# Moving dK/dV matmuls and the turns inside the attention backward loop

## The chip, the cores and the metric

The kernel runs on one core of a Trainium2 chip. The metric is the device time of one execution in microseconds, as the median of several runs. One execution was also recorded by the hardware profiler; the durations and waits quoted here come from that one.

## The reference

The reference computes a transformer block with conditioned layer norms and all its gradients: x has 2048 tokens of width 512, attention has 32 heads of width 16 without a mask, the dense part has 1792 hidden features with a squared ReLU. It returns the output and nine gradients. The change touches only the attention backward pass, which for every head computes, from the queries, keys, values and the gradient of the head's output dO:

```
P  = exp(scale * Q K^T)            (2048 x 2048 per head)
dP = dO V^T  (less the row term)    dS = P * dP
dV = P^T dO      dK = dS^T Q * scale      dQ = dS K * scale
```

The row normalisation and the row term of the softmax gradient are folded into dO before this stage: dO arrives divided by the row sums, and two more columns of dO and V carry the row term. So dS is one plain product of dP and P.

## The kernel before, in words

The kernel has three stages: the forward pass with the dense part worked in between, the attention backward pass (`attn_bwd`, from about 1170 to 2401 us of the profiled span), and the last weight gradients. Only the second is changed.

**Loops.** `attn_bwd` goes over 8 groups of four heads (`g`) and two pairs of heads in each (`jp`); one (g, jp) is called a pass here, and there are 16. A pass goes over four blocks of 512 keys (`c`), and for each over 16 blocks of 128 queries (`ib`). One (c, ib) is a unit: the two heads of the pair, 128 queries by 512 keys. Four consecutive units make a group (`i` from 0 to 3), so that a pass has 64 units and 16 groups, and the stage 1024 units. The units of a group are called first to fourth below.

**One unit.** For each of the two heads `a`, TensorE computes the scores into a one-bank PSUM tile `st` (L1584), and beside them the dP of the unit before into a tile `dp` (L1509). The two use different halves of the array's rows (64 rows each). `stp` and `dpp` have three banks each. ScalarE takes the exponential of the scores to `pu` (L1587); VectorE multiplies `dp` by the `pu` of the same unit to `ds` (L1513). Six `pu` buffers exist.

**What follows a unit.** `dS` (L1524) appends the unit to the list `pend`; when a group is complete, it issues one DMA transpose of the group's `ds` to `dsT` on SP (L1530) and appends eight dQ pieces to `pendq`. Four kinds of work are taken from lists and placed by hand between the units:

- dK and dV: `kv` (L1449) issues four matmuls with 128 contraction rows and 16 output columns each, running side by side in the array, that add to one PSUM bank `acckv`, and `kv_two` (L1494) calls it for the two oldest units. It is called at the end of the second and fourth unit of each group. When a block of keys is complete (ib 15), ScalarE evicts `acckv` to `kvT` (L1458). The next block starts a new accumulation in the same bank. Counting with the lists, the last unit of a block is worked off at the end of the fourth unit of the next block's first group.
- dQ: `dq` (L1474), 16 matmuls at the end of the first and third unit of a group, from the `dsT` of a group about two groups back. With the last piece of a pass, VectorE scales the accumulator to `dqT` (L1483).
- Turns: `turn` (L1460) transposes half of `kvT` on TensorE (8 transposes into one `st` bank, L1468) and ScalarE copies the result to `dk_t` and `dv_t` (L1472); `turn_q` (L1486) does the same for dQ (4 transposes, L1491, one copy, L1492). Both wait in the list `turnq`; one entry is taken before the second unit of a group. In an ordinary pass the three turns of the pass before fall in groups 1, 2 and 3.
- dS transposes: `turn_ds` (L1535), in even groups, transposes an eighth of the group's `ds` on TensorE and ScalarE (L1543, L1544) in place of the DMA.

**Odd groups.** `off` (L1515) holds in odd groups. There one of the eight multiplies of VectorE (second unit, second head) is left out: ScalarE copies that `dp` to SBUF (L1521) and POOL multiplies (L1522). `turn_ds` moves no data in these groups.

**What sets the order.** On TensorE, SP and POOL the instructions run in the order in which the code issues them; ScalarE's and VectorE's order in this stage follows the code as well, by the trace. So a call that is moved in the code moves in TensorE's queue. The condition on dK/dV stands in two lines:

```python
if i % 2 == 1 and len(pend) >= 4:
    kv_two()
```

When a second or fourth unit starts, `pend` has four entries, and three after `kv_two` has run; this lag is the same before and after the change.

Of the kernel before, what the change touches and what calls it, by code (L numbers as in the profile page):

```python
# [105 lines left out]
class K:  # L106
# [1322 lines left out]
    def attn_bwd(self):  # L1429
# [8 lines left out]
        S, D, H, NQ, ST, SC = self.S, self.D, self.H, self.NQ, self.ST, self.SC  # L1438
# [8 lines left out]
        pend, pendq, turnq = [], [], []  # L1447

        def kv(u):  # L1449
            (T, g, jp, c, ib, kvT, pu, ds) = u  # L1450
            for j, (n, src) in enumerate((("Q", ds), ("dO", pu))):
                for a in range(2):
                    r = 64 * j + 32 * a
                    col = (2 * jp + a) * DH
                    nc.tensor.matmul(acckv[r:r + DH, :], lhsT=T[n][:, ib, col:col + DH], rhs=src[:, a, :],  # L1455
                                     start=(ib == 0), stop=(ib == ST - 1))
            if ib == ST - 1:
                nc.scalar.activation(kvT[:, 512 * c:512 * (c + 1)], acckv[:], ACT.Copy, scale=kvs[:])  # L1458

        def turn(g, jp, kvT, s0):  # L1460

            if kvT is None:
                return turn_q(g, jp)
            h0 = 4 * g + 2 * jp
            n = ST // 2
            tp = stp.tile([P, n, P], BF16, name="st")
            for st in range(n):
                nc.tensor.transpose(tp[:, st, :], kvT[:, (s0 + st) * P:(s0 + st + 1) * P], self.ident[:])  # L1468
            v = tp[:].rearrange("p s (t a e) -> p t s a e", t=2, a=2)
            for t, dst in enumerate((self.dk_t, self.dv_t)):  # L1470
                d = dst[:, s0:s0 + n, h0 * DH:(h0 + 2) * DH].rearrange("p s (a d) -> p s a d", a=2)
                nc.scalar.copy(d, v[:, t, :, :, 0:DH])  # L1472
# [19 lines left out]
            nc.scalar.copy(self.dq_t[:, :, h0 * DH:(h0 + 2) * DH], tp[:].rearrange("p b (i e) -> p (b i) e", i=G))  # L1492

        def kv_two(n=2):  # L1494
            for u in pend[2 - n:2]:
                kv(u)
            (T, g, jp, c, ib, kvT, pu, ds) = pend[1]
            del pend[:2]
            if c % 2 and ib == ST - 1 and (g, jp) == (NQ - 1, 1):
                turnq.append((g, jp, kvT, 4 * (c - 1)))  # L1500
            elif c == SC - 1 and ib == ST - 1:
                turnq.extend((g, jp, kvT, s0) for s0 in (0, ST // 2))

        def dP(u, a):

            (T, g, jp, c, ib, kvT, pu, dsg, i, grp) = u
            rd = slice(64 - 64 * jp, 128 - 64 * jp)
            dp = dpp.tile([P, 512], F32, name="dp")
            nc.tensor.matmul(dp[:], lhsT=T["dOT"][rd, ib * P:(ib + 1) * P],  # L1509
                             rhs=masked["VT"][a][rd, 512 * c:512 * (c + 1)], start=True, stop=True)  # L1510
            if a == 1 and i == 1 and off(c, ib):
                return dp
            nc.vector.tensor_tensor(dsg[:, i, a], dp[:], pu[:, a, :], ALU.mult)  # L1513

        def off(c, ib):  # L1515
            return (c * SC + ib // G) % 2 == 1

        def dP_pool(u, dp):
            (T, g, jp, c, ib, kvT, pu, dsg, i, grp) = u
            f = (self.junk6, self.csq)[(c * SC + ib // G) // 2 % 2]  # L1520
            nc.scalar.copy(f[:], dp[:])  # L1521
            nc.gpsimd.tensor_tensor(dsg[:, i, 1], f[:], pu[:, 1, :], ALU.mult)  # L1522

        def dS(u):  # L1524

            (T, g, jp, c, ib, kvT, pu, dsg, i, grp) = u
            pend.append((T, g, jp, c, ib, kvT, pu, dsg[:, i]))
            if i == G - 1:
                dsT, n = grp
                nc.sync.dma_start_transpose(dsT[:, n:, :], dsg[:].rearrange("p i a k -> p (i a k)")[:, n * P:])  # L1530
                for a in range(2):
                    for sub in range(4):
                        pendq.append((T, g, jp, c, ib - G + 1, a, sub, dsT))
# [13 lines left out]
        T = self.T0  # L1547
        last = None
        for g in range(NQ):
            for jp in range(2):  # L1550
                if jp == 0:
                    if g + 1 < NQ:
                        Tn, later = self.load_group(g + 1)
                    else:
                        Tn, later = None, self.wq_pieces(1) + self.load_wmt()
                    cut = len(later) // 2 if Tn else len(later)
                    pieces = self.pair_pieces(g, 1) + later[:cut]
                    later = later[cut:]
                elif g + 1 < NQ:
                    pieces = self.pair_pieces(g + 1, 0) + later  # L1560
                else:
                    pieces = [(self.xhat1_6[:, st, :], self.xhat1_d.rearrange("(st p) d -> p st d", p=P)[:, st, :])
                              for st in range(ST)]
                kvT = kvp.tile([P, S], BF16, name="kvT")
                total = len(pieces)
                for c in range(SC):
                    c0 = 512 * c
                    for ib0 in range(0, ST, G):
                        m = c * (ST // G) + ib0 // G
                        while pieces and (total - len(pieces)) * SC * ST <= m * G * total:  # L1570
                            if last:
                                nc.gpsimd.tensor_copy(tick[:], last[7][0:1, 0, 0, 0:1])
                            nc.gpsimd.dma_start(*pieces.pop(0))
                        dsg, grp = self.dsp.tile([P, G, 2, 512], BF16, name="ds"), []
                        for i in range(G):
                            ib = ib0 + i
                            q = slice(ib * P, (ib + 1) * P)
                            if turnq and i == 1:
                                turn(*turnq.pop(0))
                            pu = self.pup.tile([P, 2, 512], BF16, name="pu")  # L1580
                            for a in range(2):
                                stt = stp.tile([P, 512], F32, name="st")
                                rs = slice(64 * jp, 64 * jp + 64)
                                nc.tensor.matmul(stt[:], lhsT=T["QT"][rs, q], rhs=masked["KT"][a][rs, c0:c0 + 512],  # L1584
                                                 start=True, stop=True)
                                held = dP(last, a) if last else None
                                nc.scalar.activation(pu[:, a, :], stt[:], ACT.Exp, scale=self.scale)  # L1587
                                if held is not None:
                                    dP_pool(last, held)
                            if last:  # L1590
                                dS(last)
                            last = (T, g, jp, c, ib, kvT, pu, dsg, i, grp)
                            if i % 2 == 1 and len(pend) >= 4:
                                kv_two()
                            elif i % 2 == 0 and len(pendq) > 4 * G:
                                for _ in range(8 if len(pendq) > 6 * G else 4):
                                    dq(pendq.pop(0))
                            if i == 2:
                                turn_ds(dsg, grp, off(c, ib))
            T = Tn  # L1600
        with tc.manual_schedule(engines=ALL):
            for t in (2, 0):
                for p in self.wq_pieces(t):
                    nc.gpsimd.dma_start(*p)
            for a in range(2):
                dP(last, a)
            dS(last)
            while len(pend) > 2:
                kv_two()
            kv(pend[0])  # L1610
            for _ in range(2 * G):
                dq(pendq.pop(0))
            kv_two(1)
            k0, v0, k1 = [dpp.tile([P, 512], F32, name="dp") for _ in range(3)]
            self.dw_mm(k0, 1, 0, 0, ST // 2)
            turn(*turnq.pop(0))
            for _ in range(2 * G):
                dq(pendq.pop(0))
            self.dw_mm(v0, 2, 0, 0, ST // 2)
            self.dw_mm(k0, 1, 0, ST // 2, ST)  # L1620
            self.col_sum(1)
            self.dw_mm(v0, 2, 0, ST // 2, ST)
            self.col_sum(2)
            self.cs_bc(1)
            while pendq:
                dq(pendq.pop(0))
            self.cs_bc(2)
            turn(*turnq.pop(0))
            self.dw_mm(k1, 1, 1, 0, ST)
# [312 lines left out]
```

## Time and profile before

| what | value |
|---|---|
| median of 3 runs | 2526.64 us (2521.6 to 2527.84) |
| the profiled execution's own time | 2524.31 us |
| its span, first to last instruction | 2522.4 us |
| TensorE busy | 2433.1 us, 96% of the span |
| VectorE busy | 1705.4 us, 68% |
| ScalarE busy | 2296.2 us, 91% |
| POOL busy | 713.9 us, 28% |
| multiplies dS = P dP on VectorE (L1513) | 1920, mean 681 ns |
| exponentials of the backward stage (L1587) | 2048, mean 641 ns |
| POOL's multiplies (L1522) | 128, mean 1151 to 1154 ns |

In the profile L and a number name a line of the kernel; an instruction is written as output<-inputs. PE is TensorE, PEld its weight loads, DVE is VectorE, ACT is ScalarE, SP issues the DMA transposes. The mean time of one instruction includes its overlap with the next: two multiplies in a row start closer together than 681 ns. A matmul's end is modelled, its start is recorded. In the order of time a line gives the start and the length in us, and several instructions of one kind in a row are merged and counted with x.

### The profile page before, as it was taken

How to read it: one execution, taken by the hardware profiler on the slowest of the kernel's cores; microseconds unless marked ns; L12 is line 12 of the kernel's file. 1: busy time of each engine (PE TensorE's matmuls, PEld its weight loads, DVE VectorE, ACT ScalarE, POOL GpSimd, SP SyncE). 2: the span in 40 equal slices, each digit the busy share in tenths (PEclk: the TensorE clock that was granted, in tenths of full speed). 3: DMA queues.
4: the chain of work that ended last, by engine and by line, in shares of the span. 5: the costliest groups of instructions: out<-in, count | busy, mean ns of one | idle time of the engine just before them, and what ended most of it. 6: DMA issues, size and time to landing. Idle time of an engine off the chain costs nothing.

```text
span 2522.4 us, 76903 instructions
## 1 busy us (share of the span) xinstructions
PE 2433.1 (96%) x30791; PEld 1107.9 (44%) x30791; DVE 1705.4 (68%) x3519; ACT 2296.2 (91%) x3773; POOL 713.9 (28%) x1289
## 2 busy tenths in 40 slices
PE   8999999999999999989999999999999999999998
PEld 4555555555555554673333333333333333333343
DVE  6222223422332343667999999999999999999957
ACT  7999999999999997535999999999999999999945
POOL 2344531321131022255222222222222222222223
PEclk9999999999999999999999999999999999999999
DMA  4589761441343044699999999999999999999997
GB/s 167 134 178 202 179 114 64 116 99 44 103 118 74 24 137 129 139 191 214 234 221 218 218 226 220 223 227 218 219 218 223 225 221 221 222 228 226 237 211 198
DMA packets 1260558, 446.30 MB, mean 177 GB/s; under 512 B 1204052, under 2 KB 1228246, under 8 KB 1260198
## 3 DMA queue, kind: packets, MB, share of 16 engines
q1 hardware_dynamic: 1219654, 336.29, 70.7%
q0 software_dynamic: 38464, 104.04, 13.9%
q8 instruction: 241, 3.95, 0.7%
q10 hardware_dynamic: 2080, 1.05, 0.1%
q14 instruction: 119, 0.97, 0.1%
HBM read 75.83 MB, written 64.49 MB: 56 GB/s over the span
## 4 chain that ended last, share of the span: by engine, by line
PE 59%; ACT 22%; DMA 11%; issue 4%; DVE 3%; SPq 1%; POOL 0%; DVEq 0%; ACTq 0%; POOLq 0%
ACT pu L391 18%; PE st L1584 17%; DMA dsT<-ds 8%; PE acckv L1455 8%; PE st L388 8%; PE accq L1478 5%; PE accbank L322 3%; PE dp L1509 3%; ACT pu L1587 2%; PE dps L1050 2%; PE pps L1237 2%; PE dps L995 1%; DVE ds L1513 1%; PE st L1543 1%; PE pps L631 1%
## 5 line engine op out<-in xcount | busy, mean ns | idle before, releaser
L1513 DVE TENSOR_TENSOR ds<-dp,pu 128x512 bf16<-128x512 f32 x1920 | 1178.3, 681 | 44.5 <-PE dp L1509 26.4
L1587 ACT ACTIVATE pu<-st 128x512 bf16<-128x512 f32 x2048 | 1073.9, 641 | 39.4 <-PE st L1584 21.3
L391 ACT ACTIVATE pu<-st 128x1024 bf16<-128x1024 f32 x992 | 912.2, 1077 | 5.4 <-PE st L388 5.1
L388 PE MATMUL st<-QTm,KTq 128*128 128x512 bf16 x1984 | 588.4, 377 | 19.7 <-ACT pu L391 6.1
L322 PEld LDWEIGHTS <-pu 128*128 128x128 bf16 x8192 | 347.2, 96 | 236.2 <-issue 3.2
L322 PE MATMUL accbank<-Vaug,pu 128*128 128x17 bf16 x8192 | 357.6, 171 | 1.2 <-ACT Vaug L522 0.9
L1509 PE MATMUL dp<-kvm,q 64*128 64x512 bf16 x1024 | 356.4, 382 | 2.2 <-DVE g2w L1056 0.7
L1509 PE MATMUL dp<-kvm,dOTg 64*128 64x512 bf16 x1024 | 356.2, 382 | 0.9
L1584 PE MATMUL st<-kvm,QTg 64*128 64x512 bf16 x1024 | 327.2, 381 | 10.5 <-ACT pu L1587 7.4
L1584 PE MATMUL st<-kvm,q 64*128 64x512 bf16 x1024 | 326.6, 380 | 10.8 <-ACT pu L1587 7.6
L388 PEld LDWEIGHTS <-KTq 128*128 128x128 bf16 x1984 | 188.2, 96 | 177.5 <-issue 125.9
L1522 POOL TENSOR_TENSOR ds<-junk,pu 128x512 bf16<-128x512 f32 x64 | 73.7, 1151 | 378.6 <-DVE ds L1513 336.7
L1522 POOL TENSOR_TENSOR ds<-csq,pu 128x512 bf16<-128x512 f32 x64 | 73.8, 1154 | 356.6 <-ACT csq L1521 356.6
L302 POOL DMA_DIRECT2D QTm<-QTq_d x124 | 63.5, 514 | 342.7 <-PE st L388 321.3
L1455 PE MATMUL acckv<-ds,Qg 128*16 128x512 bf16 x1024 | 154.3, 381 | 0.0
L1455 PE MATMUL acckv<-pu,dOg 128*16 128x512 bf16 x1024 | 154.2, 381 | 0.0
L1455 PE MATMUL acckv<-pu,q 128*16 128x512 bf16 x1024 | 154.0, 381 | 0.0
L1455 PE MATMUL acckv<-ds,q 128*16 128x512 bf16 x1024 | 154.0, 381 | 0.0
L329 DVE RECIPROCAL rl<-accbank 128x4 f32<-128x4 f32 x128 | 22.9, 179 | 159.5 <-PE accbank L322 159.2
L1584 PEld LDWEIGHTS <-q 64*128 64x128 bf16 x1024 | 58.1, 94 | 137.9 <-issue 104.5
L1584 PEld LDWEIGHTS <-QTg 64*128 64x128 bf16 x1024 | 57.7, 94 | 137.7 <-issue 102.7
L1509 PEld LDWEIGHTS <-q 64*128 64x128 bf16 x1024 | 88.4, 93 | 64.2 <-issue 47.4
(387 smaller groups left out, 3138.6 us busy)
## 6 DMA issues: line engine op xcount, KB each, us to landing
KTq<-KTq_d POOLq DMA_DIRECT2D x24, 512.0 KB, 3.8
duT_d<-auT POOLq DMA_DIRECT2D x3, 1792.0 KB, 8.2
aT_d<-rT POOLq DMA_DIRECT2D x3, 1792.0 KB, 11.6
KTq_d<-KTq SPq DMA_DIRECT2D x32, 128.0 KB, 2.0
QTq_d<-ev_fm SPq DMA_DIRECT2D x32, 128.0 KB, 3.4
ktm_d<-ev_tm POOLq DMA_DIRECT2D x32, 128.0 KB, 2.5
VTq_d<-vT POOLq DMA_DIRECT2D x4, 1024.0 KB, 5.8
dsT<-ds SPq DMA_TRANSPOSE x256, 7.1
```

The lines of the kernel that those rows point to most:

```text
L302: nc.gpsimd.dma_start(QTm[j][32 * j:32 * j + 32, :], self.QTq_d[g, 32 * j:32 * j + 32, 512 * qc:512 * (qc + 1)])
L322: nc.tensor.matmul(acc[:, a, sub, :], lhsT=pu[:, a, sub * P:(sub + 1) * P], rhs=Vaug[:, kb, h, :], start=(kb == 0 and a == 0 and sub == 0) ...
L388: nc.tensor.matmul(stt[:, a, :], lhsT=KT[:, kb * P:(kb + 1) * P], rhs=QTm[2 * jp + a][:], start=True, stop=True)
L391: nc.scalar.activation(pu[:], stt[:], ACT.Exp, scale=self.scale)
L1050: nc.tensor.matmul(pt[:], lhsT=a[st], rhs=g_tm[:, st, :], start=(st == 0), stop=(st == ST - 1))
L1455: nc.tensor.matmul(acckv[r:r + DH, :], lhsT=T[n][:, ib, col:col + DH], rhs=src[:, a, :], start=(ib == 0), stop=(ib == ST - 1))
L1478: nc.tensor.matmul(accq[32 * i:32 * i + 32, ib0 // G, :], lhsT=T["K"][:, 4 * c + sub, col:col + 32], rhs=dsT[:, (i * 2 + a) * 4 + sub, :], ...
L1509: nc.tensor.matmul(dp[:], lhsT=T["dOT"][rd, ib * P:(ib + 1) * P], rhs=masked["VT"][a][rd, 512 * c:512 * (c + 1)], start=True, stop=True)
L1513: nc.vector.tensor_tensor(dsg[:, i, a], dp[:], pu[:, a, :], ALU.mult)
L1522: nc.gpsimd.tensor_tensor(dsg[:, i, 1], f[:], pu[:, 1, :], ALU.mult)
L1584: nc.tensor.matmul(stt[:], lhsT=T["QT"][rs, q], rhs=masked["KT"][a][rs, c0:c0 + 512], start=True, stop=True)
L1587: nc.scalar.activation(pu[:, a, :], stt[:], ACT.Exp, scale=self.scale)
```

## The change

In odd groups, one unit's dK/dV matmuls (four) are issued between the unit's first score/dP pair and its second, in the second and fourth unit of the group, and the other four at the old place after the second pair. Even groups keep eight after the second pair. `kv_two` now takes units from the list one at a time and looks at each whether it completes a block. The turns are taken before the fourth unit of a group (`i == 3`), not before the second. After the loop the calls issue the same matmuls as before.

```diff
         def kv_two(n=2):
-            for u in pend[2 - n:2]:
+            for _ in range(n):
+                u = pend.pop(0)
                 kv(u)
-            (T, g, jp, c, ib, kvT, pu, ds) = pend[1]
-            del pend[:2]
-            if c % 2 and ib == ST - 1 and (g, jp) == (NQ - 1, 1):
-                turnq.append((g, jp, kvT, 4 * (c - 1)))
-            elif c == SC - 1 and ib == ST - 1:
-                turnq.extend((g, jp, kvT, s0) for s0 in (0, ST // 2))
+                (T, g, jp, c, ib, kvT, pu, ds) = u
+                if ib < ST - 1:
+                    continue
+                if c % 2 and (g, jp) == (NQ - 1, 1):
+                    turnq.append((g, jp, kvT, 4 * (c - 1)))
+                elif c == SC - 1:
+                    turnq.extend((g, jp, kvT, s0) for s0 in (0, ST // 2))
...
-                            if turnq and i == 1:
+                            if turnq and i == 3:
                                 turn(*turnq.pop(0))
                             pu = self.pup.tile([P, 2, 512], BF16, name="pu")
                             for a in range(2):
...
                                 nc.scalar.activation(pu[:, a, :], stt[:], ACT.Exp, scale=self.scale)
                                 if held is not None:
                                     dP_pool(last, held)
+                                if a == 0 and i % 2 == 1 and off(c, ib) and len(pend) >= 4:
+                                    kv_two(1)
                             if last:
                                 dS(last)
                             last = (T, g, jp, c, ib, kvT, pu, dsg, i, grp)
                             if i % 2 == 1 and len(pend) >= 4:
-                                kv_two()
+                                kv_two(1 if off(c, ib) else 2)
...
             while len(pend) > 2:
                 kv_two()
-            kv(pend[0])
+            kv_two(1)
             for _ in range(2 * G):
                 dq(pendq.pop(0))
             kv_two(1)
```

## The prediction

> **What bounds the kernel now.** I read the page first, then the busy time by stage, the waits of each engine in the backward stage, and VectorE's and TensorE's order of time inside one group. The page says that three engines are full in the last half, so a share of busy time can't choose between them:
>
> ```profile
> PE 2433.1 (96%) x30791; PEld 1107.9 (44%) x30791; DVE 1705.4 (68%) x3519; ACT 2296.2 (91%) x3773; POOL 713.9 (28%) x1289
> ```
>
> A 200 us stretch of the busy-time table (TensorE, its weight loads, VectorE, ScalarE, POOL, each with instructions; clock, DMA share, GB/s):
>
> ```profile
> 1300.00:1500.00 200.00, 194.21 (x2796) 68.03 (x2788) 192.24 (x315) 196.29 (x399) 51.47 (x104) 1.00 1.21 220
> ```
>
> TensorE is busy for 194 us of it, VectorE for 192, ScalarE for 196. The order of time of VectorE tells more. I call one (g, jp) a pass: 16 groups of four units, groups 0 to 15; odd groups are those where `off` holds. A unit's dP runs on TensorE beside the next unit's scores. First line below, fourth pass: from the end of group 5 through group 6 into group 7, 13 multiplies in 7.86 us; the last takes 0.68, so 12 start-to-start steps of 0.598. That is VectorE's own pace. Second: five multiplies across the odd group 7, 3.39 us, where four steps and a 0.69 tail make 3.08: 0.31 us were lost. Then two neighbours around a turn (group 2 of a later pass): 1.21 us apart.
>
> ```profile
> 1430.41 7.86 DVE L1513 TENSOR_TENSOR ds<-dp,pu 128x512 bf16<-128x512 f32 x13
> ...
> 1436.99 3.39 DVE L1513 TENSOR_TENSOR ds<-dp,pu 128x512 bf16<-128x512 f32 x5
> ...
> 2024.75 0.68 DVE L1513 TENSOR_TENSOR ds<-dp,pu 128x512 bf16<-128x512 f32 x1
> 2025.96 0.69 DVE L1513 TENSOR_TENSOR ds<-dp,pu 128x512 bf16<-128x512 f32 x1 [0.54 <-PE dp L1509]
> ```
>
> The stage runs from the first multiply at 1171.2 to the last at 2401.0, 1229.8 us. Its 1920 multiplies at 0.598 are 1148.2, fifteen dQ scalings (L1483) at 0.60 are 9.0; so 72.6 us are VectorE waiting. Spread over places by the multiplies' starts, the same in nearly every pass: odd groups lose at the first multiply of their third unit (0.11 in groups 3, 7, 11, 15, 0.19 in 5, 9, 13, 0.28 in 1) and of their fourth (0.19, 0.11, 0.08 in the same three kinds, 0.37 in 15); the two dK/dV turns lose 0.36 (group 1) and 0.62 (group 2). Sums: 1.29 + 1.35 + 0.98 = 3.6 us a pass, some 57 us in 16. The rest follows late dsT transfers.
>
> The waits of the stage agree on who is late: VectorE waits for dP, rarely for ScalarE; TensorE's dQ matmuls waited 22 times for the dsT transfers.
>
> ```profile
> DVE ds L1513 <- PE dp L1509: 26.4, 62, 2.0
> DVE ds L1513 <- ACT pu L1587: 3.1, 11, 0.3
> ...
> PE accq L1478 <- DMA dsT<-ds: 13.8, 22, 2.1
> ```
>
> Why dP is late in odd groups is seen on TensorE, units 2 to 4 of group 7:
>
> ```profile
> 1437.13 0.37 PE L1509 MATMUL dp<-kvm,dOTg 64*128 64x512 bf16 x1
> 1437.43 0.41 PE L1478 MATMUL accq<-dsT,Kg 128*32 128x128 bf16 x16
> 1437.77 0.39 PE L1584 MATMUL st<-kvm,QTg 64*128 64x512 bf16 x1
> 1437.77 0.39 PE L1509 MATMUL dp<-kvm,dOTg 64*128 64x512 bf16 x1
> 1438.00 0.38 PE L1584 MATMUL st<-kvm,QTg 64*128 64x512 bf16 x1
> 1438.32 0.37 PE L1509 MATMUL dp<-kvm,dOTg 64*128 64x512 bf16 x1
> 1438.63 0.39 PE L1455 MATMUL acckv<-ds,Qg 128*16 128x512 bf16 x2
> ...
> 1438.85 0.38 PE L1455 MATMUL acckv<-ds,Qg 128*16 128x512 bf16 x2
> ...
> 1439.17 0.39 PE L1509 MATMUL dp<-kvm,dOTg 64*128 64x512 bf16 x1
> ```
>
> From 1437.77 the second score follows after 0.23, but its dP only after 0.55: it stands 0.32 us for a free dp bank (three banks; the multiply three back starts at 1437.59 and ends at 1438.27). Only then come the eight dK/dV matmuls, and the next dP, at 1439.17, is 0.85 behind. From a dP's start to its multiply takes 0.52 (1437.77 to 1438.30, 1439.17 to 1439.69). VectorE was free 0.19 before.
>
> **What the skill says.** "TensorEngine Tiling (Array Packing)", Key Properties: changing the tiling mode drains TensorE. The trace agrees: dP to dK/dV (64-row to 128x32 tiles) starts after 0.30, back after 0.32, inside dK/dV the step is 0.22. "Perfetto Trace Analysis", Identifying the Most-Contended Engine: matmul busy time is no measure of TensorE's headroom; here it hides the 0.32 wait. The same page, Optimization Strategy: a bubble that repeats can mean too few buffers; the repeated 0.19 and the wait for one of three dp banks fit.
>
> **The change, part by part.**
>
> *1. The split in odd groups.* No instruction is added or removed. At unit 2 and 4 TensorE's order pair, pair, 8 dK/dV becomes pair, 4, pair, 4. Length without waits: before 0.23 + 0.85 = 1.08; after, pair to pair across four is 0.30 + 0.32 = 0.62, so 1.24. The two extra mode changes cost 0.16 to 0.17 us of TensorE. In group 7 they fall into the 0.32 wait: second dP at 1437.77 + 0.62 = 1438.39 (0.07 later; its multiply is due at 1438.91, and 1438.39 + 0.52 meets that), next dP at 1439.01 for 1439.17. That dP's multiply could start at 1439.53; VectorE is ready at 1439.51. So 0.19 shrinks to 0.02 or 0.03: gain 0.16. The 0.11 before stays: the dP ahead waited for VectorE's bank at 1437.07, then 16 dQ matmuls. Groups 7, 11, 15: 0.16 each (in 15 the other 0.18 stays).
> Groups 5, 9, 13 come after a kvT eviction. In group 5, unit 2's second score waits 0.34 for ScalarE until 1426.83; four dK/dV now run before it, so unit 3's first dP moves from 1427.69 to 1427.45, the next is held by VectorE's bank until 1427.85 (1427.92 before), dQ and the following dP 1428.49 for 1428.57: gain 0.07. Unit 4: dP at 1428.49 + 1.24 = 1429.73 for 1429.89, multiply 0.02 late where it was 0.11: 0.09 or so more. Together 0.17.
> Added wait: the early four open a new accumulation in group 1, 5, 9, 13 and must wait for the eviction. It ends at 1425.59 + 0.70 = 1426.29, and 1426.10 + 0.30 = 1426.40 is their earliest start. Behind them stand the second score and dP, which wait for an exp that is itself behind the eviction. Price 0; if it came late, its delay. The Pool-made dS piece (ends 1440.01) is read at 1440.96, then 1440.80: covered.
>
> *2. Turns from unit 2 to unit 4.* A dK/dV turn is 8 transposes and two ScalarE copies: dQ block to next dP grows from 0.34 to 0.89, 0.55 (2024.79 to 2025.34); the dQ turn adds 0.33 (four transposes). ScalarE pays the same copies (0.53 and 0.48 in pitch) either way. Walking a pass without transfer stalls:
> No DMA and nothing of SP or POOL is in a turn, and it passes none of theirs.
> Group 1: the place ahead of unit 2 loses the turn, 0.36 becomes 0. The place ahead of unit 4 gains it: the loss there (third unit's first multiply) was 0.28, in an odd group where one multiply is Pool's; bank release + 0.06 + 0.64 (dQ) + 0.55 + 0.52 = 1.8 against two multiplies, 1.2: loss 0.63 to 0.66. With the 0.08 after it gone the group ends 0.06 ahead. The turn's st bank comes back with its second copy, by the walk 0.05 to 0.1 before the third score after it.
> Group 2: 0.62 ahead of unit 2 goes. Ahead of unit 4, dQ, four dS transposes (0.33) and the turn put dP 1.5 after the one before; but the dQ scaling (0.60) stands in VectorE's queue just there, so four steps, 2.4, cover 1.5 + 0.06 + 0.52 = 2.1. Loss 0, gain 0.62. Without that cover it would be 0.3.
> Group 3: the dQ turn was free ahead of unit 2; ahead of unit 4 it adds 0.33 to the 0.11; the split wins its 0.16. Net -0.17 or so.
> Sum 0.51 a pass, 15 passes (the first has no turns, and wins 0.3 by the split; the last pass's extra turn in group 9 moves too, 0.3 at most).
>
> *3. The ring behind.* Groups of a pass become shorter by 1.5 in 76.9 us. dsT lands a median 7.1 us after its issue and is used two groups (9.1) later; a tenth of the groups have under 0.06 us to spare, the median 0.9. Two groups shrink by 0.18: the 22 waits grow by that (4 us), about 25 more begin at half of it (2), and of TensorE's waits VectorE has so far passed on half to three quarters. Cost 3, between 0 and 8.
>
> *Sum:* 16 x (3 x 0.16 + 3 x 0.17) = 15.8; 15 x 0.51 = 7.7; 0.3; less 3: 20.8, say 21 us. Span 2522.4 becomes 2501; the profiled execution's own 2524.3 becomes 2503; the median of runs lies 2.3 higher, 2526.6, and I take the difference there: **2505.6**, 0.8% less. Unknown ends: the group 1 turn could lose 0.3 more or less (5 us in all), mode changes in the new order 0.5 to 1.5 times those seen (10 us). A comparison of this kernel can tell about 0.3%, 7.6 us.
>
> **Rivals.**
> *TensorE's mode changes decide.* If the second pair of unit 2 or 4 doesn't wait, 0.167 per split stays on the path: two an odd group, 128 odd groups: 43 us, less some 6 that the turns of group 2 give: near 2563. It decides from a wait under 0.17 in most places. For: TensorE 194 of 200 us. Against: the waits seen are 0.28 (unit 2), 0.32 (unit 4), 0.25 to 0.34 in group 5.
> *The transfers take it.* With dsT late, TensorE waits there instead, hidden gain: about 2522. For: 22 waits, the transpose queue's packets at 115% of the 16 engines' time (1420 to 1500), 3.9 to 4.2 us of issue on SP in each 4.6 us. Against: median margin 0.9.
> *ScalarE is the bound.* Four groups cost it 32 exps x 0.477 + 4 copies x 0.465 + an eviction 0.57 = 17.7 us, VectorE 30 x 0.598 = 17.9, measured 18.5. Turns add 1.6 in groups 0 to 3. If exps start late after the moved copies, the turns' gain goes: about 2515.
>
> **How the numbers follow.** Forecast case 0.72 (2492 to 2514); ScalarE 0.11 (2511 to 2519); transfers 0.09 (2519 to 2527); mode changes 0.08 (2534 to 2563). The range 2493 to 2520 leaves out the last case, half of the third, and tails. Faster 0.83, same 0.09, slower 0.08.
>
> **What would show it.** Right: in group 7, 4 + 4 matmuls with dP 0.62 apart, and the 5 multiplies of 3.39 at about 3.22; VectorE's lost time in the stage near 50 us; 0.6 lost in group 1 and 0.44 in group 3 at the third unit's first multiply, only the 0.6 of the dQ scaling in group 2. Wrong, too, if the turn of group 1 costs over 1 us there. Else: the third unit's losses grow in odd groups (rival 1), many more than 22 waits for dsT (2), VectorE waiting for pu (3).

## The result and the profile after

The changed kernel takes 2513.66 us in the median of 7 runs (2510.12 to 2517.87), beside 2522.75 us for the kernel before on the same chip: a ratio of 0.9965, 95% interval 0.9953 to 0.9978, 9.1 us less. Measured again later beside other kernels it was 2521.91 beside 2526.73 us, 0.9975 (0.9962 to 0.9989); that ratio is not the one of the two medians, which lie 4.8 us apart (0.9981). Faster was right; 0.8% was forecast, 0.25 to 0.35% came.

The page of the changed kernel, and the same 200 us of its busy-time table (columns as before):

```profile
PE 2437.6 (97%) x30791; PEld 1133.6 (45%) x30791; DVE 1708.5 (68%) x3519; ACT 2297.0 (91%) x3773; POOL 715.9 (28%) x1289
```

```profile
1300.00:1500.00 200.00, 195.75 (x2816) 72.70 (x2808) 193.98 (x317) 197.87 (x402) 51.10 (x105) 1.00 1.19 222
```

The instruction counts are unchanged. In the same 200 us VectorE runs 317 instructions for 315: that is the gain, and busy shares can't show more of it.

TensorE's order of time in the same place as before, units 3 and 4 of group 7 of the fourth pass:

```profile
1431.72 0.39 PE L1511 MATMUL dp<-kvm,dOTg 64*128 64x512 bf16 x1
1432.03 0.39 PE L1455 MATMUL acckv<-ds,Qg 128*16 128x512 bf16 x2
...
1432.36 0.39 PE L1511 MATMUL dp<-kvm,dOTg 64*128 64x512 bf16 x1
1432.68 0.39 PE L1455 MATMUL acckv<-ds,Qg 128*16 128x512 bf16 x2
...
1433.01 0.39 PE L1511 MATMUL dp<-kvm,dOTg 64*128 64x512 bf16 x1
```

From 1431.72 the dPs follow at 1432.36 and 1433.01. The two steps are 0.65 and 0.64, together 1.29 us; before they took 0.55 and 0.85, 1.40. The wait for a dp bank is filled, as forecast, but the steps are 0.645 in the trace and not 0.62.

VectorE over the same group, the five multiplies that took 3.39 us before:

```profile
1430.94 3.29 DVE L1515 TENSOR_TENSOR ds<-dp,pu 128x512 bf16<-128x512 f32 x5
```

3.29 where 3.22 was forecast: 0.11 lost as before at the third unit's first multiply, and now 0.05 at each of the next two. And the turn of group 1, in a later pass:

```profile
2010.78 1.28 DVE L1515 TENSOR_TENSOR ds<-dp,pu 128x512 bf16<-128x512 f32 x2
2012.63 0.69 DVE L1515 TENSOR_TENSOR ds<-dp,pu 128x512 bf16<-128x512 f32 x1 [0.58 <-ACT junk L1523]
```

The second of the two on the first line starts at 2011.37; the next comes 1.26 later, 0.66 over VectorE's own step. The forecast was 0.63 to 0.66. The view names a copy of ScalarE as what ended the wait, because that copy ends at 2012.63 as well. The dP of this multiply explains the time without it: it stands behind the turn's transposes on TensorE, and from its start to the multiply are 0.52 us, as before the change:

```profile
2011.56 0.62 PE L1468 MATMUL st<-ident,kvT 128*128 128x128 bf16 x8
...
2012.11 0.39 PE L1511 MATMUL dp<-kvm,dOTg 64*128 64x512 bf16 x1
```

Such losses can be summed. A pass has 120 places for a multiply on VectorE (8 in an even group, 7 in an odd one). For each I take the start of the multiply less that of the one before, less 0.598; the median over the 16 passes is the place's regular loss, and what the passes differ from it is irregular. Over the stage, in us (the runs with one part alone are described below):

| lost by VectorE | before | after | split alone | turns alone |
|---|---|---|---|---|
| odd groups, third unit, first multiply, groups 5 to 15 | 14.1 | 11.1 | 12.0 | 15.8 |
| the same, groups 1 and 3 | 6.1 | 17.9 | 8.3 | 19.4 |
| odd groups, third unit, second multiply | 1.3 | 5.9 | 6.0 | 1.3 |
| odd groups, fourth unit, first multiply | 21.0 | 8.9 | 8.9 | 16.2 |
| groups 1 and 2, first unit (turns before) | 16.0 | 1.0 | 15.7 | 1.0 |
| other even groups, first unit | 0.4 | 3.2 | 3.0 | 1.8 |
| dQ scaling (its own 0.60) | 9.6 | 9.6 | 9.6 | 9.6 |
| rest | 2.3 | 1.3 | 1.3 | 2.2 |
| regular, sum | 70.7 | 58.8 | 64.7 | 67.0 |
| irregular | 11.6 | 14.4 | 13.5 | 11.5 |

The regular part falls by 11.9 us, the irregular part rises by 2.8; the stage of the profiled execution is 9.1 us shorter (1220.8 for 1229.8), which is the difference of the medians too. In the second profiled execution of the same kernel the regular part is 58.5, the irregular 24.8. So the regular part repeats, and the irregular one carries the scatter from execution to execution.

Most of the difference between the two executions is TensorE's granted clock, the share of full speed that it was given. The second execution was the slowest of its nine runs (2530.98 us), and three stretches of 6.8 us in its stage ran at half clock; in the first execution's stage there is none. Their sum, length times the share that was not granted, is 10.2 us, and the irregular parts differ by 10.4. The same 40 us of both, the first execution ahead (columns as before):

```profile
2285.00:2325.00 40.00, 37.95 (x546) 13.80 (x544) 37.58 (x62) 38.81 (x79) 10.07 (x20) 1.00 1.28 228
...
2285.00:2325.00 40.00, 33.84 (x428) 10.96 (x425) 29.95 (x49) 30.28 (x60) 7.53 (x15) 0.83 1.15 202
```

With a clock of 0.83 on the mean VectorE runs 49 instructions where it ran 62.

The waits of the stage after:

```profile
DVE ds L1515 <- PE dp L1511: 26.4, 57, 1.2
...
PE accq L1478 <- DMA dsT<-ds: 15.5, 30, 1.3
```

VectorE still waits for dP, and TensorE for dsT, 30 times for 22. The wait of TensorE's scores for ScalarE's exp (14.9 us, 44 times before) is down to one of 0.2 us.

### The profile page after: what moved, and what is told of

It is laid out like the page before. It is cut to its first block, busy times and chain, and to the rows that moved or that the text cites. A ratio compares the mean times of both kernels' runs of the same rounds, so it can differ in the third digit from the quotient of the medians.

```text
span 2513.3 us, 76903 instructions
## 1 busy us (share of the span) xinstructions
PE 2437.6 (97%) x30791; PEld 1133.6 (45%) x30791; DVE 1708.5 (68%) x3519; ACT 2297.0 (91%) x3773; POOL 715.9 (28%) x1289
## 4 chain that ended last, share of the span: by engine, by line
PE 55%; ACT 24%; DMA 12%; issue 4%; DVE 3%; POOL 0%; SPq 0%; DVEq 0%; ACTq 0%; POOLq 0%
ACT pu L391 19%; PE st L1586 15%; DMA dsT<-ds 10%; PE st L388 8%; PE acckv L1455 7%; PE accq L1478 5%; ACT pu L1589 4%; PE accbank L322 3%; DVE ds L1515 2%; PE dps L1050 2%; PE pps L1237 2%; PE dp L1511 1%; PE st L1545 1%; PE dps L995 1%; PE pps L631 1%
## 5 line engine op out<-in xcount | busy, mean ns | idle before, releaser
L1511 PE MATMUL dp<-kvm,q 64*128 64x512 bf16 x1024 | 363.5, 384 | 1.3 <-DVE g2w L1056 0.7
L1586 PE MATMUL st<-kvm,q 64*128 64x512 bf16 x1024 | 349.9, 381 | 4.7 <-ACT pu L1589 0.2
L1586 PE MATMUL st<-kvm,QTg 64*128 64x512 bf16 x1024 | 349.4, 381 | 4.0
L1455 PE MATMUL acckv<-ds,Qg 128*16 128x512 bf16 x1024 | 176.2, 382 | 0.0
L1455 PE MATMUL acckv<-pu,dOg 128*16 128x512 bf16 x1024 | 175.9, 382 | 0.0
L1455 PE MATMUL acckv<-pu,q 128*16 128x512 bf16 x1024 | 175.8, 382 | 0.0
L1455 PE MATMUL acckv<-ds,q 128*16 128x512 bf16 x1024 | 175.8, 382 | 0.0
L1586 PEld LDWEIGHTS <-q 64*128 64x128 bf16 x1024 | 66.9, 93 | 141.0 <-issue 108.8
L1586 PEld LDWEIGHTS <-QTg 64*128 64x128 bf16 x1024 | 66.6, 93 | 141.0 <-issue 108.0
L1478 PE MATMUL accq<-dsT,Kg 128*32 128x128 bf16 x4096 | 105.5, 221 | 10.5 <-DMA dsT<-ds 10.2
## 6 DMA issues: line engine op xcount, KB each, us to landing
aT_d<-rT POOLq DMA_DIRECT2D x3, 1792.0 KB, 11.1
```

What stands on the lines that cost most here:

```text
L1478: nc.tensor.matmul(accq[32 * i:32 * i + 32, ib0 // G, :], lhsT=T["K"][:, 4 * c + sub, col:col + 32], rhs=dsT[:, (i * 2 + a) * 4 + sub, :], ...
```

## The experiments

Four questions: which part carries the gain; whether the turns are well placed; what sets the 0.05 that was not forecast; whether the late transfers can be got rid of. Each run was measured beside the kernel before.

### The parts alone

The split without the turns:

```diff
-                            if turnq and i == 3:
+                            if turnq and i == 1:
```

> The split of dK/dV in odd groups as in the change, the turns where they were. Theory, place by place on TensorE: the split wins some 0.8 us a pass at the fourth unit's first multiply (12.5 us), gives back 2 at the third unit and 2 to late dsT transfers: 8 us less than before, 7 to 10. Losses of the turns stay 0.36 in group 1 and 0.62 in group 2. Rival, the moved turns carry the gain: within 2 us of before.

Measured: 2521.61 beside 2524.42, ratio 0.9992 (0.9983 to 1.0000). The rival's "within 2 us of before" is nearer than the 8 us. The table shows why. The fourth unit's multiply wins its 12.1 us, as expected. But 4.7 come back at the third unit's second multiply, 2.6 at even groups' first unit, and groups 1 and 3 lose 2.2 more. And 15.7 us stay lost at the turns.

The turns without the split:

```diff
-                                if a == 0 and i % 2 == 1 and off(c, ib) and len(pend) >= 4:
-                                    kv_two(1)
...
-                                kv_two(1 if off(c, ib) else 2)
+                                kv_two()
```

> The turns ahead of the fourth unit, dK/dV unsplit in all groups. Theory: 0.36 and 0.62 a pass disappear in groups 1 and 2, about 0.37 and 0.33 appear at the third unit's first multiply of groups 1 and 3: 0 to 4 us less than before. Rival, the moved turns carry the gain: 9 us less.

Measured: 2521.56, 0.9991 (0.9980 to 1.0003): within the 0 to 4 us. 15.0 us vanish in groups 1 and 2, 13.3 appear at the third unit of groups 1 and 3. The medians give 3 us for each part and 5 to 9 for both; the regular parts 6.0, 3.7 and 11.9. Neither carries the gain alone, and each is at the edge of what can be told from no change.

Which of the two splits counts:

```diff
-                                if a == 0 and i % 2 == 1 and off(c, ib) and len(pend) >= 4:
+                                if a == 0 and i == 3 and off(c, ib) and len(pend) >= 4:
                                     kv_two(1)
...
-                                kv_two(1 if off(c, ib) else 2)
+                                kv_two(1 if off(c, ib) and i == 3 else 2)
```

(with the turns ahead of the second unit)

> The split only in the fourth unit of odd groups, the second unit keeps its eight after both pairs; turns where they were. Theory: only the fourth unit's split feeds a multiply that VectorE waits for, so 8 to 11 us less than before, as with both. If the second unit's split carries half, 4 to 5 us less. If mode changes cost at the second unit, this is the faster of the two by 2 us or more.

Measured: 2520.29, 0.9984 (0.9975 to 0.9993): 4 us less than before, half of the expectation and about as both splits. Its fourth unit's multiply loses 8.9 us, as with both. So the split of the second unit adds nothing in the sum: the regular part is 63.9 us here and 64.7 with both splits. But the reason given for that was not right. Place by place the second unit's split does feed multiplies that VectorE waits for: with it, the third unit's first multiply loses 0.07 to 0.08 less in groups 5, 9 and 13. It gives this back as 0.10 more in group 3 and 0.03 to 0.05 at the first unit of groups 6, 10 and 14. The size of the gain falls short for the same reason as above.

### Where a turn is cheap

```diff
-                            if turnq and i == 3:
+                            if turnq and i == 1 and not off(c, ib):
```

> The changed kernel, with turns taken ahead of the second unit of even groups alone (groups 2, 4 and 6). Theory: a turn is covered where three multiplies lie between the release of the dp bank and the next one needed, so 0.67 of group 1 and 0.33 of group 3 disappear, at most 0.1 each appears: 10 to 15 us less than the changed kernel, 19 to 24 less than before. Rival, a turn costs TensorE its 0.55 us wherever it stands: no change against the changed kernel, 9 less than before.

Measured: 2527.85, 1.0014 (1.0004 to 1.0025), 3 us more than before. The expectation failed. Group 2 still loses 0.61 ahead of its second unit, group 4 loses 0.32 and group 6 0.38. VectorE around the turn of group 4 in this run, and TensorE ahead of it:

```profile
1420.66 1.29 DVE L1515 TENSOR_TENSOR ds<-dp,pu 128x512 bf16<-128x512 f32 x2
1422.18 0.69 DVE L1515 TENSOR_TENSOR ds<-dp,pu 128x512 bf16<-128x512 f32 x1 [0.23 <-PE dp L1511]
```

```profile
1420.36 0.38 PE L1511 MATMUL dp<-kvm,dOTg 64*128 64x512 bf16 x1
1420.66 0.41 PE L1478 MATMUL accq<-dsT,Kg 128*32 128x128 bf16 x16
1421.00 0.62 PE L1468 MATMUL st<-ident,kvT 128*128 128x128 bf16 x8
...
1421.56 0.39 PE L1511 MATMUL dp<-kvm,dOTg 64*128 64x512 bf16 x1
```

I had counted three multiplies from the release of a bank as cover. TensorE was not there at the release: at the end of an odd group it comes just in time with every dP (the 0.05 show it), so the cover is what lies ahead of the dP at 1420.36, not of the release. A turn needs a place where TensorE is ahead, and that is the end of an even group:

```diff
-                            if turnq and i == 3:
+                            if turnq and i == 3 and not off(c, ib):
```

> The changed kernel with turns taken ahead of the fourth unit of even groups alone (groups 2, 4, 6). Theory now: TensorE has no lead over VectorE at the end of an odd group and has built it up by the end of an even one, so the turn in group 2 costs nothing (the dQ scaling covers it), the one in group 4 0.3 us, the dQ turn in group 6 0.1, for 1.1 a pass in the changed kernel: about 10 us less than the changed kernel, 19 less than before. Rival, a turn costs its TensorE time wherever it stands: no change against the changed kernel.

Measured: 2518.7, 0.9986 (0.9974 to 0.9997). Group 2 costs nothing and group 4 0.29, as expected, but group 6 costs 0.26 and another 0.15 one unit on, and group 5 loses 0.33 at its third unit, where the changed kernel loses 0.13. Regular part 59.6, as in the changed kernel (58.8 and 58.5); the time is no better. The rival, that a turn's time on TensorE comes up again wherever it stands, fits but for group 2, where the dQ scaling covers it.

### The dQ block and the pace of the split

```diff
+                                if a == 0 and i == 2 and off(c, ib) and len(pendq) > 4 * G:
+                                    for _ in range(8 if len(pendq) > 6 * G else 4):
+                                        dq(pendq.pop(0))
...
-                            elif i % 2 == 0 and len(pendq) > 4 * G:
+                            elif i % 2 == 0 and not (i == 2 and off(c, ib)) and len(pendq) > 4 * G:
```

> The changed kernel, with the 16 dQ matmuls of the third unit of odd groups issued between its two score and dP pairs. No mode change is added. Theory: the third unit's first multiply waits 0.11 to 0.13 because the dP ahead of the dQ block is held by a dp bank; with dQ in that wait it comes in time, 0 to 0.03 lost, so 0.09 a group in 128 groups, and with a little given back to late transfers 8 to 12 us less than the changed kernel. Rival, the loss only moves to the next multiply, which waits for the same bank: 0 to 3 us less.

Measured: 2518.12, 0.9983 (0.9976 to 0.9991), no better than the changed kernel. In group 7 the third unit's first multiply now loses 0.01 where it lost 0.11, and the next one 0.08 where it lost 0.05; groups 5, 9 and 13 lose 0.10 to 0.12 at the fourth unit, and even groups 0.04 to 0.10 at their first. Against the 5.9 us won at the third unit's first multiply in groups 5 to 15 stand 4.4 more lost at the fourth unit and 5.9 in even groups; the regular part is 62.7 for 58.8. The rival was right: the loss moves on.

The price of the split where it isn't needed:

```diff
-                                if a == 0 and i % 2 == 1 and off(c, ib) and len(pend) >= 4:
+                                if a == 0 and i % 2 == 1 and len(pend) >= 4:
                                     kv_two(1)
...
-                                kv_two(1 if off(c, ib) else 2)
+                                kv_two(1)
```

> The changed kernel, with the split in even groups too. Theory: each split is 0.21 us longer on TensorE; even groups have some 0.5 us to spare and lose 0.42 of it, so TensorE enters the odd groups without a lead: 5 to 20 us more than the changed kernel. Rival, mode changes are hidden everywhere: no change. Fully exposed: 54 us more.

Measured: 2528.59, 1.0017 (1.0006 to 1.0027); some 11 to 13 us more than the changed kernel, by the difference of the ratios (0.0052 or 0.0042 of 2523 us). Mode changes aren't hidden everywhere, nor fully exposed. Its regular part is 71.6, 13 above the changed kernel's.

What sets the 0.05 was tried by making the four matmuls shorter. In odd groups they run over 256 of the 512 columns; half of that part of dK and dV is not computed in this run (but for the first query block):

```diff
-        def kv(u):
+        def kv(u, w=512):
...
-                    nc.tensor.matmul(acckv[r:r + DH, :], lhsT=T[n][:, ib, col:col + DH], rhs=src[:, a, :],
+                    nc.tensor.matmul(acckv[r:r + DH, :w], lhsT=T[n][:, ib, col:col + DH], rhs=src[:, a, :w],
...
-                                    kv_two(1)
+                                    kv_two(1, 256)
...
-                                kv_two(1 if off(c, ib) else 2)
+                                kv_two(*((1, 256) if off(c, ib) else (2,)))
```

> The changed kernel beside the other three, on one chip: 7 to 11 us less than before.

> The changed kernel, with the dK/dV matmuls issued in odd groups over 256 of their 512 columns (half of their work is left out, except for the first query block, which is whole). Theory: a dP follows the one before across four dK/dV matmuls after 0.645 us where VectorE's step is 0.598, which is the 0.05 lost at the third unit's second and the fourth unit's first multiply in every odd group; with half the columns it follows after 0.54, and both losses vanish: 0.1 x 128, 8 to 13 us less than the changed kernel, less what late transfers take of it. Rival, the 0.05 are a fixed wait on semaphores: no change at those two places.

Measured on one chip: the changed kernel 2521.91 and this 2514.12 beside 2526.73 (0.9975 and 0.9942, the latter 0.9927 to 0.9957): 7.8 us less than the changed kernel. TensorE and VectorE in group 7 of this run:

```profile
1432.23 0.39 PE L1511 MATMUL dp<-kvm,dOTg 64*128 64x512 bf16 x1
1432.55 0.28 PE L1455 MATMUL acckv<-ds,Qg 128*16 128x256 bf16 x2
...
1432.78 0.37 PE L1511 MATMUL dp<-kvm,dOTg 64*128 64x512 bf16 x1
1433.09 0.28 PE L1455 MATMUL acckv<-ds,Qg 128*16 128x256 bf16 x2
...
1433.31 0.39 PE L1511 MATMUL dp<-kvm,dOTg 64*128 64x512 bf16 x1
```

```profile
1431.45 3.19 DVE L1515 TENSOR_TENSOR ds<-dp,pu 128x512 bf16<-128x512 f32 x5
```

The steps are 0.55 and 0.53, under VectorE's 0.598, and the five multiplies take 3.19: the 0.11 at the third unit's first multiply is left, and the other two losses are 0.01 and 0.00. So the 0.05 is the pace of the order pair, four, pair itself, 0.645 for 0.598, and no fixed wait. The regular part is 51.2 for 58.5, 7.3 less, just under the 8 to 13 expected, because groups 6, 10 and 14 now lose 0.10 at their first unit, where they lost 0.05 or less.

### The matmuls moved to the even group

If a split in odd groups is too long, one unit's four matmuls can go into the next even group, where they stand ahead of the dQ matmuls:

```diff
+                            if i == 0 and not off(c, ib) and len(pend) >= 5:
+                                kv_two(1)
                             if i % 2 == 1 and len(pend) >= 4:
-                                kv_two(1 if off(c, ib) else 2)
+                                kv_two(1 if off(c, ib) and i == 3 else 2)
...
+            if len(pend) > 4:
+                kv_two(1)
             while len(pend) > 2:
                 kv_two()
```

(no split; turns ahead of the second unit as before)

> Turns as before; no split. In odd groups the fourth unit issues one unit's four dK/dV matmuls after both pairs; the other four go to the end of the first unit of the next even group, ahead of its dQ matmuls, where no mode change is added. Theory: in odd groups the fourth unit's first multiply comes in time (0 to 0.03 lost, 0.11 to 0.19 before) without the 0.645 pace, the third unit's first keeps 0.11 to 0.19, even groups have the time: 12 to 18 us less than before, 3 to 9 less than the changed kernel; if transfers take what the odd groups win, 0 to 5 less than before.

Measured: 2528.81, 1.0009 (1.0000 to 1.0017). The fourth unit's multiply comes in time in all odd groups but the last of a pass (2.5 us lost for 21.0), and the even groups' first unit loses 23.8 us where it lost 0.4. Before group 10 in this run:

```profile
1447.62 1.28 DVE L1515 TENSOR_TENSOR ds<-dp,pu 128x512 bf16<-128x512 f32 x2
1449.08 0.69 DVE L1515 TENSOR_TENSOR ds<-dp,pu 128x512 bf16<-128x512 f32 x1 [0.17 <-PE dp L1511]
```

```profile
1447.58 0.39 PE L1511 MATMUL dp<-kvm,dOTg 64*128 64x512 bf16 x1
1447.90 0.39 PE L1455 MATMUL acckv<-ds,Qg 128*16 128x512 bf16 x2
...
1448.12 0.40 PE L1478 MATMUL accq<-dsT,Kg 128*32 128x128 bf16 x16
1448.45 0.39 PE L1511 MATMUL dp<-kvm,dOTg 64*128 64x512 bf16 x1
```

The multiply at 1449.08 is 0.26 late, because its dP stands behind four plus sixteen matmuls, 0.87 us. The even group has the time, but only later, and its first unit is too early to use it. The same with one turn in group 2 and two in groups 3 and 7:

```diff
-                            if turnq and i == 3:
+                            if turnq and ((c == 0 and ib0 == 2 * G and i == 3) or (ib0 == 3 * G and i == 1)):
```

> As the run with the four moved matmuls, and one turn ahead of the fourth unit of group 2, where the dQ scaling covers it, the next two ahead of the second unit of groups 3 and 7, at the end of an even group, where TensorE is ahead. Theory: the 0.36 of group 1 and the 0.62 of group 2 vanish, at most 0.3 a pass appears in groups 3 and 7: 8 to 12 us less than that run, 20 to 28 less than before. Rival, the turn's time on TensorE shows up in any odd group: 2 to 5 us less than that run.

Measured: 2521.96, 0.9981 (0.9972 to 0.9990): 6.9 us less than the run before it, a little under the 8 to 12. Groups 1 and 2 lose 4.3 us at their first unit for 19.9; the turns in groups 3 and 7 cost 0.16 and 0.03 there, but the groups behind them, 4 and 8, lose 0.11 and 0.15 more at their first unit than in the run before. So a good part of a turn's time shows up one group later, and the 20 to 28 us less than before were far too many: 4.8 came. It is level with the changed kernel on that chip (2521.91). No version tried that does all the work beats it clearly.

### Late transfers

```diff
-                            elif i % 2 == 0 and len(pendq) > 4 * G:
-                                for _ in range(8 if len(pendq) > 6 * G else 4):
+                            elif i % 2 == 0 and len(pendq) > 5 * G:
+                                for _ in range(8 if len(pendq) > 7 * G else 4):
```

> The changed kernel, with every dQ piece taken half a group later, so that a dsT transfer has 2.3 us more. Theory: the irregular losses at the first multiply of groups 0, 6, 8, 10, 11, 12, 14, some 0.7 us a pass above their medians, come from late transfers and vanish: 8 to 11 us less; the dQ scaling leaves group 2, where its turn then costs about 0.3 a pass (5 us) : together 3 to 8 us less than the changed kernel. Rival, the irregular losses are not from the transfers: 5 us more.

Measured: 2527.26 (2515.76 to 2545.84), 1.0018 (1.0006 to 1.0030): slower than before, against the expectation. The profiled execution is the fastest of its 22 runs, and even there the irregular part is 12.8 us. VectorE's and TensorE's waits for others in its stage:

```profile
DVE ds L1515 <- PE dp L1511: 21.2, 53, 0.8
DVE ds L1515 <- DMA dsT<-ds: 6.6, 10, 2.2
```

```profile
PE dp L1511 <- DVE ds L1515: 11.7, 27, 1.8
```

TensorE's dQ no longer waits for dsT at all; VectorE does instead, ten times, up to 2.2 us, and TensorE behind it. The output `ds` of a group goes to one of three buffers, which the transfer must have read before VectorE writes it again: that is how I read the wait, and it wasn't tried with a fourth buffer. `dsT` has four buffers, which the later dQ holds half a group longer, and that can delay the transfers; this wasn't tried either. So the run doesn't tell whether late transfers make the irregular losses: it moved the wait and didn't remove it. What makes this kernel's median so much worse than its profiled execution stays open.

In the 14 profiled executions the irregular part is mostly the larger the smaller the regular one. The granted clock has a share in that: eight of them have one to three stretches of 3.4 or 6.8 us at half clock in the stage. The six without such a stretch show the rest: 6.7 us irregular at 80.5 regular (the moved matmuls), 9.3 at 71.6 (split in all groups), 11.6 at 70.7 (before), 13.5 at 64.7 and 14.2 at 63.9 (the split alone, in both units and in the fourth), 14.4 at 58.8 (the changed kernel). A straight line through these six has a slope of -0.4.

The medians of the runs, which don't hang on one execution, agree. In the 13 comparisons with the kernel before, the time goes with the regular part by a line of slope 0.5 to 0.6; single kernels lie up to 8 us off it, the last run most. So of a microsecond won from VectorE's regular waits about half reached the median, and the rest came back in places that change from execution to execution.

TensorE's waits for dsT grow as the regular part falls: 6.4 us (the moved matmuls), 7.5 (split in all groups), 13.8 (before), 15.5 and 17.9 (the changed kernel), 25.3 (half columns), but none in the last run. That the transfers cause the loss is argued from these waits and not shown; no run here took the transfers away, and the one that gave them more time was slower. "DMA: Bandwidth & Descriptors" of the Trainium skill, Latency and other measured facts, gives an effective 261 GB/s for DMA transposes with a non-contiguous middle dimension and some 350 to 400 for contiguous ones; this kernel moves 222 GB/s in the 200 us above, its other loads included, at or near the same rate in every stretch of the stage, and no run here shows where its ceiling lies.

## Why the prediction was right, and where it was too large

**Right: what bounds the stage.** VectorE at 0.598 a step, held up by dP in odd groups and at turns. The regular losses stayed in odd groups and at turns but for 3.2 us at the first unit of even groups, and shortening TensorE's block in odd groups moved the time (half columns, 7.8 us).

**Right: the turns.** Forecast for group 1 0.63 to 0.66, found 0.67 (median); group 3 0.44, found 0.44; group 2 nothing but the dQ scaling, found so. Summed, groups 1 and 2 at their first unit win 15.0 us and the third unit of groups 1 and 3 loses 11.8. One sum is written loosely: for group 1, 0.06 + 0.64 + 0.55 + 0.52 is 1.77, and 1.2 taken from it leaves 0.57. The 0.66 comes out when the cover is counted from the release of the bank, at a multiply's end: three steps less its 0.68 us, 1.11.

**Wrong by size: "pair to pair across four is 0.30 + 0.32 = 0.62".** It is 0.645. Both figures lie above VectorE's 0.598, but 0.62 only by 0.02. I had put these two pieces together from places where eight matmuls stand and had checked the sum only against the dP bank; the lines shown there give 0.31 + 0.32 already (1438.32, 1438.63; 1438.85, 1439.17). In the changed kernel the medians over all such places are 0.320 from the pair to the first of the four, 0.010 to the last of the four, and 0.315 to the next pair. Two such steps in a row pace VectorE. The forecast of 0.02 or 0.03 lost in each odd group became two times 0.05. The fourth unit's multiply was to win 15.9 us by the sum's own terms and won 12.1; the third unit's second multiply was to stay and lost 4.6; even groups begin up to 0.05 late (groups 6, 10 and 14 among them), 2.8 in all. Together 11.2 of the 11.9 us between the 23.8 forecast for the regular part and the 11.9 found. The groups after an eviction, forecast to win 0.17 each, won 0.09 to 0.10 (0.318 to 0.229 in group 5), from the same term.

**Signs that failed.** The five multiplies of group 7 take 3.29 us where 3.22 was named, and VectorE's lost time in the stage, 72.6 before, is 63.6 (58.8 + 14.4 less the 9.6 of the dQ scaling) where some 50 was named.

**Transfers: cost 3, between 0 and 8.** The profiled execution shows 2.8 more irregular loss. From the regular part, 11.9 us less, the runs kept 9.1 on one chip and 4.8 to 6.3 on the other, so 3 to 7 us did not arrive. That is inside the range, but that the transfers took all of it isn't shown. The second execution's irregular part can't be charged to them, as half clock took 10.2 us there; the working had no term for the clock.

**Luck in the absolute time.** The forecast counted its 21 us from 2526.6. Beside the changed kernel the kernel before took 2522.75, so 3.9 us of the nearness of 2513.66 to 2505.6 come from a lower start and not from the gain. On the other chip the changed kernel took 2521.91, above the 2520 at which the range ends.

**The rivals.** Mode changes were named as the way to a slower kernel, decided where the second pair waits less than 0.17. They did not decide, but they are the part that was underpriced: where the split isn't needed it costs 11 to 13 us. TensorE waits for transfers 30 times for 22, 1.7 us longer in all, so they didn't take the whole gain. ScalarE was not the bound: VectorE's waits for `pu` fell from 3.1 us to 0.2.

## What to carry to other kernels

When two engines run in step with a few banks between them, price a reordering by the longest step it makes between two results, and compare that with the consumer's own step: below it the order is free, and above it the excess is paid at every step. A block that is moved out of a tight stretch needs a place where the producer is ahead, not merely one with spare time later. And take a gain that is summed from one engine's regular waits as an upper end: here about half of it reached the median of the runs, and what took the other half was not shown.

## What the runs showed of the hardware

Between matmuls of different array tiling the start-to-start time is 0.30 to 0.33 us, where two blocks of the same tiling follow after 0.22 to 0.23: 0.08 to 0.11 us for each change of tiling, with 512 moving columns. With 256 columns between two such changes a block of four takes 0.53 to 0.55 from pair to pair where it takes 0.645 with 512. From the pair to the four it is 0.32 in both; only from the four to the next pair it falls, from 0.315 to 0.21. So the change itself costs the same, and the 256 columns, 0.1 us, are what is saved. Four matmuls of 16 output columns each in different column tiles start within 0.01 us of each other.

The granted clock of TensorE falls to half for 3.4 or 6.8 us at a time: no such stretch in the stage of six of the 14 profiled executions, one or two of 3.4 us in seven, three of 6.8 us in one. What sets them off was not looked into.
